# One float32 score product per head instead of three split ones, a later weight conversion, and two small passes on ScalarE

## The chip, the cores and the metric

The kernel runs on one core of a Trainium2 chip. The metric is the device time of one execution in microseconds. A core has a matrix engine (PE, whose weight loads are listed as PEld), a vector engine (DVE), a scalar engine (ACT), GpSimd (POOL), and SyncE (SP), which here issues the DMAs. Each engine works through its own queue in order.

## The reference

Attention with a compressive memory, and then two feed-forward layers, all in float32:

```
B, H, S, D = 4, 8, 576, 64
scores = q k^T / 8, causal;  a = softmax(scores);  local = a v
q_p = phi(q) = max(q, 0) + exp(min(q, 0))
mem_out = (q_p M_prev) / (q_p z_prev + 1e-6)
g = sigmoid(beta);  x = g * mem_out + (1 - g) * local     # 2304 tokens x 512
h = x w1_in (512 x 2048);  x = (h * cos(h)) w1_out
h = x w2_in (512 x 2048);  out = (h * tanh(softplus(h))) w2_out
```

## The kernel before

**Number format.** The kernel multiplies large matrices as pairs of float32r tiles, a rounded high part and the rest as a low part: a product a b is formed as aH bH + aH bL + aL bH, three matmuls into the same PSUM bank. Transposes, the memory product, a v and the sum with the memory's part are plain float32 products; the trace has two records (weight load and matmul) for each plain float32 product that isn't a transpose.

**Stages.** `attention` works on pairs of heads, 16 of them (4 batches of 4 pairs). The 576 query rows of a pair are 5 steps, i=0 to 4, so 80 steps in all, 20 per batch. In steps i=0 to 3 each head has its own score tile of 128 rows and 128(i+1) columns, and the two heads' operands lie in rows 0 to 63 and 64 to 127 of the array. Step 4 holds the last 64 rows of both heads in one tile (512 columns and 64 more). A step has three parts: `stage_a` (scores, softmax), two steps later `stage_b` (transposes of the attention tile), four steps later `stage_c` (a v, the sum, and the split into xH and xL, which are stored to DRAM with step 4).

**prep (L198 to L230)** runs for the next pair with step i=3. It loads k and q (kd, qd, from three shared `raw` tiles), rounds them to kh and qh, subtracts to kl and ql, and computes phi into `ph`: a minimum with 0 on DVE (L224), an exponential on ACT (L225), and one DVE pass (L226). `TURNS` gives the engine of each small operation in turn ("v" DVE, "a" ACT, "p" POOL), with own entries for the first batch (names that end in 0).

**stage_a (L232 to L275).** The three products per head (L246, L260), a custom DVE pass that adds the mask and takes the row's extreme (L248, L262, L265), the exponential on ACT that also gives the row sum sm (L251, L267), 1e-9 added to sm on DVE (L271), the reciprocal on DVE (L272), and the scaling of the tile on POOL (L274).

**The feed-forward** runs in three sequences: m1 (half of layer 1's hidden columns, blocks of 256 tokens), m2 (the other half) and m3 (layer 2). m1 is issued between attention's steps from the second batch on, by a pace (L580 to L586); what is left of it follows attention. In a unit the first product is L429, the second L487 (L496 in m3).

**The weight conversion.** Weights arrive in DRAM as 64 bit numbers. `to_f32` (L119 to L132) loads a piece of 512 KB into one of two staging tiles (`wst`) and turns it into float32 by one pass on POOL (L117), one on ACT (L126) and three on DVE (L127, L128, L131). `load_half` then rounds it into the high tile (ACT or POOL) and subtracts into the low tile (L161, POOL or DVE). The first half of layer 1 has 16 pieces. They are issued with attention's steps: after step s, int((s - CONV0 + 1) * CONVR) pieces, and at the latest before the units that need them (L584).

**Order.** The written order is the priority of a scheduler that simulates the engines and fixes each engine's queue, so that instructions can stand earlier or later than written; `issue_after` ties a piece behind the exponential of its step.

Of the kernel before, what the change touches and what calls it, by code (L numbers as in the profile page):

```python
# [9 lines left out]
F32 = mybir.dt.float32  # L10
F32R = mybir.dt.float32r
# [10 lines left out]
    mb=2, raw=3, aD=4, kh=3, kl=3, qs=2, vt=2, qt=1, ph=2, den=2, mo=4, xH=1, xL=3, sm=7, mn=2, at=8, aT=7, u=2, e=3, g=4, h=4, y=4, xb=3, yp=3, yh=2, yl=2, wst=2, S=6, T=8,  # L22
# [3 lines left out]
CONV0 = 2  # L26
CONVR = 1.5
# [6 lines left out]
    sc0="p", ql0="vp", kh0="a", kl0="vp", qh0="a", aT0="a",  # L34
    sc="p", ql="vp", kh="p", kl="ppv", ws="p", w0l="pv", w1l="vp", w2l="vp", w3l="vp", gl="p", gh="v", bh="a", mh="a",
    wh="ap", aT="av", yl="p", ml="vp", y0="v", y1="a", qh="a", aD="v",
# [7 lines left out]
def attention_moe_moe_kernel(  # L44
# [41 lines left out]
    make_identity(nc, ident)  # L86
    c_hpi = const.tile([P, 1], F32, name="c_hpi")
# [16 lines left out]
    def turn_of(kind, first=False):  # L104
        kind += "0" if first else ""
        n = counts.get(kind, 0)
        counts[kind] = n + 1
        return {"a": nc.scalar, "p": nc.gpsimd, "v": nc.vector}[TURNS[kind][n % len(TURNS[kind])]]
# [67 lines left out]
    def attention(ap, pools):  # L176
# [21 lines left out]
        def prep(b, p):  # L198
            st = {}

            kd = ap.tile([P, S + D], F32, tag="raw", name="kd", bufs=BUFS["raw"])
            kd = kd[:, :S]
            nc.sync.dma_start(kd, kT[b, p])
            qd = ap.tile([P, S + D], F32, tag="raw", name="qd", bufs=BUFS["raw"])
            nc.sync.dma_start(qd, qT[b, p])
            kh = ap.tile([P, S], F32R, tag="kh", name="kh", bufs=BUFS["kh"])
            kl = ap.tile([P, S], F32R, tag="kl", name="kl", bufs=BUFS["kl"])
            qh = ap.tile([P, S + D], F32R, tag="qh", name="qh", bufs=BUFS["qs"])
            ql = ap.tile([P, S + D], F32R, tag="ql", name="ql", bufs=BUFS["qs"])
            scaled("kh", kh, kd, first=b == 0)  # L210
            scaled("qh", qh, qd, first=b == 0)
            turn_of("kl", b == 0).tensor_tensor(kl, kd, kh.bitcast(F32), ALU.subtract)
            turn_of("ql", b == 0).tensor_tensor(ql, qd, qh.bitcast(F32), ALU.subtract)
            st["terms"] = ((qh, kh), (ql, kh), (qh, kl))
# [9 lines left out]
            nc.vector.tensor_scalar(ph, qt, 0.0, None, ALU.min)  # L224
            nc.scalar.activation(ph, ph, AF.Exp)  # L225
# [6 lines left out]
        def stage_a(b, p, i):  # L232
# [7 lines left out]
            if i < 4:  # L240
                N = P * (i + 1)
                sps = [bank("S", [P, SM], "sp") for _ in range(2)]
                for m, (q_, k_) in enumerate(st["terms"]):
                    for j, sp in enumerate(sps):
                        rows = slice(j * D, (j + 1) * D)
                        nc.tensor.matmul(sp[:, :N], q_[rows, q0:q0 + P], k_[rows, :N], start=m == 0, stop=m == 2)  # L246
# [7 lines left out]
            else:  # L254
                N = S
                at = ats[0]
                for k0, k1, w, name in ((0, SM, SM, "sp"), (SM, S, D, "sd")):
                    out = bank("S", [P, SM], name)
                    for m, (q_, k_) in enumerate(st["terms"]):
                        nc.tensor.matmul(out[:, :w], q_[:, q0:q0 + P], k_[:, k0:k1], start=m == 0, stop=m == 2)  # L260
                    if k0 == 0:
                        nc.vector.tensor_tensor_reduce(  # L262
                            at[:, :SM], out, mask[:, 0:SM], SSC, 3.0e38, ALU.add, ALU.min, mn[:, 0:1])
                    else:
                        nc.vector.tensor_tensor_reduce(  # L265
                            at[:, SM:], out[:, :D], mask2, SSC, mn[:, 0:1], ALU.add, ALU.min, mn[:, 1:2])
# [4 lines left out]
            nc.vector.scalar_tensor_tensor(sm, sm, 1e-9, sm, ALU.add, ALU.max)  # L271
# [404 lines left out]
```

## Time and profile before

| | |
|---|---|
| runs | 1080.91, 1084.23, 1088.42 us, median 1084.23 |
| profiled execution | 1085.15 us, its span 1083.4 us, mean granted clock 0.987 |
| PE, PEld busy | 1051.3 us (97 %), 901.1 us (83 %) |
| DVE, ACT, POOL busy | 531.2 us (49 %), 474.2 us (44 %), 434.3 us (40 %) |

The span is the time from the first to the last instruction. Busy times are unions over an engine's instructions; the sums of single lines can be larger, because neighbours overlap. Matmul ends are modelled, so a busy PE need not be PE at its peak. Attention ends at about 395 us, m1 at about 500 us, m2 at about 680 us.

### The profile page before, as it was taken

What the parts mean: (1) busy time and instruction counts of PE and PEld (TensorE: products, weight loads), DVE (VectorE), ACT (ScalarE), POOL (GpSimd) and SP (SyncE); (2) the same over time, 40 slices, a digit from 0 to 9 for tenths busy, and PEclk for the clock granted to TensorE, in tenths of its full rate; (3) what the DMA queues carried; (4) which work ended last, traced back from release to release, by engine and by line L of the source; (5) the groups of instructions that cost most, each with busy time, mean ns of one, the idle gap of its engine ahead of it and who ended that gap; (6) DMA issues with size and microseconds to landing.
All of it is one profiled execution on the core that took longest, in us unless ns stands there. A gap on an engine that the chain in (4) does not pass through costs nothing.

```text
span 1083.4 us, 17564 instructions
## 1 busy us (share of the span) xinstructions
PE 1051.3 (97%) x6672; PEld 901.1 (83%) x6672; DVE 531.2 (49%) x1246; ACT 474.2 (44%) x947; POOL 434.3 (40%) x454
## 2 busy tenths in 40 slices
PE   7888899999999999999999999999999999999998
PEld 5667688898989899998888889888888888888897
DVE  7999885647483657766657564655100000000000
ACT  6777475637273634334454454534422222232231
POOL 5988562435333335445556465544210101010100
PEclk9999799999999999999999999999999999999999
DMA  6566442424231246434456345633300200110010
GB/s 220 177 198 194 140 140 76 140 61 135 66 97 34 82 168 213 128 100 134 147 175 204 127 155 163 220 114 97 117 1 1 91 26 1 58 39 1 20 40 20
DMA packets 66373, 117.04 MB, mean 108 GB/s; under 512 B 5616, under 2 KB 25072, under 8 KB 66288
## 3 DMA queue, kind: packets, MB, share of 16 engines
q1 hardware_dynamic: 66288, 115.91, 32.7%
q8 instruction: 53, 0.87, 0.3%
q14 instruction: 32, 0.26, 0.1%
HBM read 87.58 MB, written 28.31 MB: 107 GB/s over the span
## 4 chain that ended last, share of the span: by engine, by line
PE 80%; DVE 7%; ACT 5%; DMA 4%; issue 2%; POOL 1%; SPq 0%; ACTq 0%; POOLq 0%; DVEq 0%
PE h L429 33%; PE y L496 18%; PE y L487 16%; PE o L333 3%; PE tp L306 3%; PE sp L246 3%; DMA wst<-in_w1i_dram 1%; DMA wst<-in_w1o_dram 1%; PE mp L286 1%; PE o L322 1%; DVE wst L131 1%; ACT at L251 1%; DVE wst L127 1%; DVE w L161 1%; DVE at L248 1%
## 5 line engine op out<-in xcount | busy, mean ns | idle before, releaser
L429 PE MATMUL h<-xbH,w 128*128 128x256 f32 (+1 forms) x1536 | 394.6, 338 | 0.2 <-DMA xbH<-xsH 0.2
L429 PEld LDWEIGHTS h<-xbH,w 128*128 128x128 f32 x1536 | 267.1, 190 | 33.6 <-issue 1.2
L429 PE MATMUL h<-xbL,w 128*128 128x256 f32 (+1 forms) x768 | 258.3, 337 | 0.0
L487 PE MATMUL y<-g,w 128*128 128x256 f32 (+1 forms) x1344 | 223.9, 321 | 1.7 <-DVE g L115 1.0
L487 PEld LDWEIGHTS y<-g,w 128*128 128x128 f32 x1344 | 195.7, 195 | 22.7 <-issue 3.3
L496 PE MATMUL y<-w,g 128*128 128x512 f32 x864 | 201.8, 389 | 0.0
L496 PEld LDWEIGHTS y<-w,g 128*128 128x128 f32 x864 | 161.9, 188 | 33.5
L401 DVE TENSOR_TENSOR g<-e,g 128x512 fp32r<-128x512 f32 x36 | 25.3, 702 | 288.9 <-ACT g L113 258.4
L429 PEld LDWEIGHTS h<-xbL,w 128*128 128x128 f32 x768 | 145.6, 190 | 15.5 <-DMA xbL<-xsL 0.3
L401 POOL TENSOR_TENSOR g<-e,g 128x512 fp32r<-128x512 f32 x36 | 47.6, 1322 | 275.6 <-ACT g L113 275.6
L274 POOL TENSOR_SCALAR at<-at,sm,omg 128x128 f32<-128x128 f32 (+2 forms) x144 | 110.2, 777 | 83.9 <-DVE sm L272 51.1
L393 ACT ACTIVATE e<-h 128x512 f32<-128x512 f32 x72 | 42.8, 595 | 216.7 <-PE h L429 216.3
L401 POOL TENSOR_TENSOR g<-u,g 128x512 fp32r<-128x512 f32 x72 | 102.3, 1438 | 70.7 <-DVE g L115 51.7
L117 POOL TENSOR_SCALAR wst<-wst 128x512 f32<-128x512 f32 x64 | 45.6, 713 | 116.7 <-DMA wst<-in_w2i_dram 40.6
L376 ACT ACTIVATE u<-h 128x512 int32<-128x512 f32 x72 | 42.3, 594 | 97.0 <-PE h L429 85.8
L251 ACT ACTIVATE at<-at,mn 128x128 f32<-128x128 f32 (+3 forms) x128 | 71.0, 556 | 30.7 <-DVE mn L248 28.3
L126 ACT ACTIVATE wst<-wst,c_seven 128x512 int32<-128x512 uint32 x64 | 48.9, 766 | 68.6 <-DMA wst<-in_w1o_dram 19.6
L306 PE MATMUL tp<-ident,at 128*128 128x128 f32 x384 | 67.3, 295 | 7.8 <-DVE xL L338 3.7
L377 DVE SCALAR_TENSOR_TENSOR u<-u,h 128x512 f32<-128x512 int32 x72 | 49.0, 683 | 51.0 <-ACT u L376 50.8
L127 DVE SCALAR_TENSOR_TENSOR wst<-wst 128x512 int32<-128x512 int32 x64 | 50.0, 781 | 41.6 <-ACT wst L126 20.4
L131 DVE TENSOR_TENSOR wst<-wst 128x512 int32<-128x512 int32 x64 | 68.4, 1070 | 1.1
L333 PE MATMUL o<-aT,vt 128*64 128x128 f32 (+1 forms) x896 | 63.9, 273 | 0.0
(94 smaller groups left out, 1251.5 us busy)
## 6 DMA issues: line engine op xcount, KB each, us to landing
wst<-in_w1i_dram SPq DMA_DIRECT2D x16, 512.0 KB, 3.9
wst<-in_w1o_dram SPq DMA_DIRECT2D x16, 512.0 KB, 4.1
wst<-in_w2i_dram SPq DMA_DIRECT2D x16, 512.0 KB, 3.7
wst<-in_w2o_dram SPq DMA_DIRECT2D x16, 512.0 KB, 3.6
qd<-in_qT_dram SPq DMA_DIRECT2D x16, 320.0 KB, 3.2
vt<-in_vn_dram SPq DMA_DIRECT2D x16, 320.0 KB, 3.3
xbH<-xsH SPq DMA_DIRECT2D x20, 256.0 KB, 4.6
xbL<-xsL SPq DMA_DIRECT2D x20, 256.0 KB, 4.4
```

What stands on the lines that cost most here:

```text
L126: nc.scalar.activation(lo, lo.bitcast(U32), AF.Relu, scale=-(2.0 ** -29), bias=c_seven)
L127: nc.vector.scalar_tensor_tensor(lo, hi, 3, lo, ALU.logical_shift_left, ALU.bitwise_or)
L131: nc.vector.tensor_tensor(dst, lo, hi, ALU.bitwise_xor)
L251: marks["act"] = nc.scalar.activation(at[:, :N], at[:, :N], AF.Exp, bias=mn[:, j:j + 1], scale=-1.0, accum_out=sm[:, j:j + 1]).ins
L274: turn_of("sc", b == 0).tensor_scalar(at[:, :N], at[:, :N], sm[:, j:j + 1], gates[j], ALU.mult, ALU.mult)
L306: nc.tensor.transpose(tp[:, c:c + P], at[:, c:c + P], ident)
L333: marks["pe"] = nc.tensor.matmul(o[j * D:(j + 1) * D, :n], st["vt"][:kk, c, j * D:(j + 1) * D], a, start=False, stop=c == i, skip_group_ch ...
L377: nc.vector.scalar_tensor_tensor(u, u.bitcast(I32), -TWO_PI, h, ALU.mult, ALU.add)
L401: turn_of(kind).tensor_tensor(gL, g, gH.bitcast(F32), ALU.subtract)
L429: nc.tensor.matmul(h[:, a * T:(a + 1) * T], w_[:, c, f0:f0 + P], x_[c], start=m == 0, stop=m == 3 * NC - 1)
L487: nc.tensor.matmul(y[e // per][:, cols], w_[:, f, es], g_, start=fst and m == 0 and e % per == 0, stop=lst and m == 2, skip_group_check=True)
L496: nc.tensor.matmul(y[t], g_[:, tsl], w_[:, f, :], start=fst and m == 0, stop=lst and m == 2, skip_group_check=True)
```

## The change

- Scores become one plain float32 product of q and k per head (steps 0 to 3) or per column range (step 4). The rounded and low tiles kh, kl, qh, ql and the operations that make them are gone. kd and qd are read by the matmuls themselves and have four tiles each; the three `raw` tiles are gone.
- The first weights' conversion starts with step 14 (CONV0) and issues 0.9 pieces a step (CONVR), instead of from step 2 with 1.5.
- phi's minimum, a DVE pass, becomes a Relu of -q on ACT, and the exponential takes the sign: exp(-relu(-q)).
- The 1e-9 on the row sum is added by an Identity pass with a bias tile on ACT, not by DVE.

```diff
-    mb=2, raw=3, aD=4, kh=3, kl=3, qs=2, vt=2, ...
+    mb=2, kd=4, qd=4, aD=4, vt=2, ...
-CONV0 = 2
-CONVR = 1.5
+CONV0 = 14
+CONVR = 0.9
 TURNS = dict(
-    sc0="p", ql0="vp", kh0="a", kl0="vp", qh0="a", aT0="a",
-    sc="p", ql="vp", kh="p", kl="ppv", ws="p", ...
+    sc0="p", aT0="a",
+    sc="p", ws="p", ...
...
+    c_eps = const.tile([P, 1], F32, name="c_eps")
+    nc.gpsimd.memset(c_eps, 1e-9)
...
-            kd = ap.tile([P, S + D], F32, tag="raw", name="kd", bufs=BUFS["raw"])
-            kd = kd[:, :S]
+            kd = ap.tile([P, S], F32, tag="kd", name="kd", bufs=BUFS["kd"])
             nc.sync.dma_start(kd, kT[b, p])
-            qd = ap.tile([P, S + D], F32, tag="raw", name="qd", bufs=BUFS["raw"])
+            qd = ap.tile([P, S + D], F32, tag="qd", name="qd", bufs=BUFS["qd"])
             nc.sync.dma_start(qd, qT[b, p])
-            kh = ap.tile([P, S], F32R, tag="kh", name="kh", bufs=BUFS["kh"])
-            kl = ap.tile([P, S], F32R, tag="kl", name="kl", bufs=BUFS["kl"])
-            qh = ap.tile([P, S + D], F32R, tag="qh", name="qh", bufs=BUFS["qs"])
-            ql = ap.tile([P, S + D], F32R, tag="ql", name="ql", bufs=BUFS["qs"])
-            scaled("kh", kh, kd, first=b == 0)
-            scaled("qh", qh, qd, first=b == 0)
-            turn_of("kl", b == 0).tensor_tensor(kl, kd, kh.bitcast(F32), ALU.subtract)
-            turn_of("ql", b == 0).tensor_tensor(ql, qd, qh.bitcast(F32), ALU.subtract)
-            st["terms"] = ((qh, kh), (ql, kh), (qh, kl))
+            st["q"], st["k"] = qd, kd
...
-            nc.vector.tensor_scalar(ph, qt, 0.0, None, ALU.min)
-            nc.scalar.activation(ph, ph, AF.Exp)
+            nc.scalar.activation(ph, qt, AF.Relu, scale=-1.0)
+            nc.scalar.activation(ph, ph, AF.Exp, scale=-1.0)
...
-                for m, (q_, k_) in enumerate(st["terms"]):
-                    for j, sp in enumerate(sps):
-                        rows = slice(j * D, (j + 1) * D)
-                        nc.tensor.matmul(sp[:, :N], q_[rows, q0:q0 + P], k_[rows, :N], start=m == 0, stop=m == 2)
+                for j, sp in enumerate(sps):
+                    rows = slice(j * D, (j + 1) * D)
+                    nc.tensor.matmul(sp[:, :N], st["q"][rows, q0:q0 + P], st["k"][rows, :N], start=True, stop=True)
...
-                    for m, (q_, k_) in enumerate(st["terms"]):
-                        nc.tensor.matmul(out[:, :w], q_[:, q0:q0 + P], k_[:, k0:k1], start=m == 0, stop=m == 2)
+                    nc.tensor.matmul(out[:, :w], st["q"][:, q0:q0 + P], st["k"][:, k0:k1], start=True, stop=True)
...
-            nc.vector.scalar_tensor_tensor(sm, sm, 1e-9, sm, ALU.add, ALU.max)
+            nc.scalar.activation(sm, sm, AF.Identity, bias=c_eps)
```

## Rows read from the trace of the kernel before

**Rows 1.** Windows: start:end, length, busy us (instructions) by engine, granted clock, DMA share, GB/s.

```profile
0.00:20.00 20.00, 11.95 (x53) 9.12 (x54) 13.55 (x46) 11.90 (x28) 11.04 (x36) 1.00 0.74 249
20.00:160.00 140.00, 124.53 (x1045) 98.89 (x1045) 129.44 (x401) 96.72 (x262) 105.35 (x113) 0.94 0.53 167
160.00:400.00 240.00, 236.72 (x2071) 210.28 (x2072) 137.57 (x460) 125.82 (x291) 86.98 (x106) 0.98 0.28 90
500.00:1084.00 584.00, 579.78 (x2738) 487.48 (x2737) 180.31 (x232) 201.69 (x313) 179.11 (x152) 1.00 0.26 87
```

**Rows 2.** Chain that ended last, 0 to 160 us: start us, us, what.

```profile
24.68 0.86 ACT at L267 x2
...
68.00 1.69 DVE wst L131
...
141.07 0.87 ACT at L267 x2
```

**Rows 3.** Timeline of ACT near 59 us: start us, us, instruction, shapes, count.

```profile
59.09 0.79 ACT L267 ACTIVATE at<-at,mn 128x576 f32<-128x576 f32 x1
```

**Rows 4.** Lines on DVE, 0 to 160 us: count | busy us, mean ns | idle before.

```profile
L131 DVE TENSOR_TENSOR wst<-wst 128x512 int32<-128x512 int32 x16 | 16.2, 1010 | 0.0
L271 DVE SCALAR_TENSOR_TENSOR sm<-sm 128x2 f32<-128x2 f32 (+1 forms) x40 | 16.1, 403 | 1.9 <-ACT at L251 1.9
L127 DVE SCALAR_TENSOR_TENSOR wst<-wst 128x512 int32<-128x512 int32 x16 | 12.0, 750 | 0.7 <-POOL wst L117 0.6
L128 DVE TENSOR_SCALAR wst<-wst 128x512 int32<-128x512 int32 x16 | 9.6, 599 | 0.0
L161 DVE TENSOR_TENSOR w<-wst,w 128x512 fp32r<-128x512 f32 x8 | 9.1, 1137 | 0.5 <-POOL w L117 0.5
L213 DVE TENSOR_TENSOR ql<-qd,qh 128x640 fp32r<-128x640 f32 x5 | 5.3, 1063 | 0.1
L224 DVE TENSOR_SCALAR ph<-qt 128x576 f32<-128x576 f32 x10 | 5.2, 518 | 1.2 <-DMA qt<-in_qp_dram 1.2
L212 DVE TENSOR_TENSOR kl<-kd,kh 128x576 fp32r<-128x576 f32 x4 | 3.4, 857 | 1.0 <-ACT kh L113 1.0
```

**Rows 5.** Lines on ACT, 0 to 160 us.

```profile
L113 ACT ACTIVATE qh<-qd 128x640 fp32r<-128x640 f32 x10 | 7.3, 731 | 3.5 <-PE sd L260 3.4
L225 ACT ACTIVATE ph<-ph 128x576 f32<-128x576 f32 x10 | 6.7, 674 | 0.4 <-DVE ph L224 0.2
L94 ACT ACTIVATE gate<-gate 128x8 f32<-128x8 f32 x1 | 0.2, 208 | 0.7 <-DMA gate<-in_beta_dram 0.7
```

**Rows 6.** Lines on POOL, 0 to 160 us.

```profile
L212 POOL TENSOR_TENSOR kl<-kd,kh 128x576 fp32r<-128x576 f32 x7 | 10.8, 1536 | 8.0 <-ACT kh L113 7.8
L213 POOL TENSOR_TENSOR ql<-qd,qh 128x640 fp32r<-128x640 f32 x5 | 8.0, 1594 | 0.4 <-ACT qh L113 0.4
```

**Rows 7.** Timeline of PE, 53 to 62 us: scores, and float32 products in column halves.

```profile
53.77 0.44 PE L333 MATMUL o<-aT,vt 128*64 128x128 f32 x4
...
56.24 0.66 PE L333 MATMUL o<-aT,vt 128*64 128x128 f32 x8
...
56.99 0.28 PE L246 MATMUL sp<-kh,ql 64*128 64x128 f32 x2
57.10 0.28 PE L246 MATMUL sp<-kl,qh 64*128 64x128 f32 x2
...
60.05 0.41 PE L246 MATMUL sp<-kh,ql 64*128 64x512 f32 x2
60.28 0.41 PE L246 MATMUL sp<-kl,qh 64*128 64x512 f32 x2
```

**Rows 8.** Tile wst, 0 to 160 us: durations min/median/max ns, first and last start us.

```profile
L161 DVE TENSOR_TENSOR w<-wst,w x8: 668/680/3995, 29.9 to 141.2; 128x512 fp32r<-128x512 f32 x8
```

**Rows 9.** Waits of SP's DMA queue, 0 to 160 us: total us, times, longest.

```profile
SPq L123 <- POOL w L161: 13.8, 6, 5.3
...
SPq L203 <- POOL ql L213: 6.4, 2, 3.4
```

More of the change, by code (lines that the diff above doesn't have):

```diff
@@ L21 @@
 BUFS = dict(
-    mb=2, raw=3, aD=4, kh=3, kl=3, qs=2, vt=2, qt=1, ph=2, den=2, mo=4, xH=1, xL=3, sm=7, mn=2, at=8, aT=7, u=2, e=3, g=4, h=4, y=4, xb=3, yp=3, yh=2, yl=2, wst=2, S=6, T=8,
+    mb=2, kd=4, qd=4, aD=4, vt=2, qt=1, ph=2, den=2, mo=4, xH=1, xL=3, sm=7, mn=2, at=8, aT=7, u=2, e=3, g=4, h=4, y=4, xb=3, yp=3, yh=2, yl=2, wst=2, S=6, T=8,
 )
@@ L33 @@
 TURNS = dict(
-    sc0="p", ql0="vp", kh0="a", kl0="vp", qh0="a", aT0="a",
-    sc="p", ql="vp", kh="p", kl="ppv", ws="p", w0l="pv", w1l="vp", w2l="vp", w3l="vp", gl="p", gh="v", bh="a", mh="a",
-    wh="ap", aT="av", yl="p", ml="vp", y0="v", y1="a", qh="a", aD="v",
+    sc0="p", aT0="a",
+    sc="p", ws="p", w0l="pv", w1l="vp", w2l="vp", w3l="vp", gl="p", gh="v", bh="a", mh="a",
+    wh="ap", aT="av", yl="p", ml="vp", y0="v", y1="a", aD="v",
 )
```

## The prediction

> **What bounds the kernel now.** I read the profile by stretches first, because its whole-span shares mix stages with different limits. The windows [rows 1] show that from 160 us to the end the matrix engine PE is the limit: 237 of 240 us busy up to 400 us, then 100 %, with DVE, ACT and POOL far below. Before 160 us it is another machine: between 20 and 160 us DVE is busy 129.4 of 140 us (92 %), PE 124.5, POOL 105, ACT 97. Busy PE time is a modelled latency there; the mean granted clock of that stretch, 0.94, is a mixture of the two levels, 1.2 and 2.4 GHz. So PE starves for a good part of this stretch, and what starves it is DVE.
>
> The chain of waits tells the same [rows 2]: it runs through DVE's pieces of the weight conversion (L131 at 68 us, 1.69 us, is one of these links). It also gives the pace of attention: the exponential of step i=4 of the first pair starts at 24.7 us, that of the seventh pair at 141.1 us, so (141.1 - 24.7)/6 = 19.4 us a pair. The timeline of ACT puts the third pair's, which is step 14, at 59.1 us [rows 3].
>
> What fills DVE up to 160 us is in its lines [rows 4]: four lines of conversion make 16.2 + 12.0 + 9.6 + 9.1 = 46.9 us. The four lines that the change takes off DVE make 16.1 (L271) + 5.3 (L213) + 5.2 (L224) + 3.4 (L212) = 30.0 us. Line sums overlap on the engine: all DVE lines of the stretch together make 172 us where the windows give 13.55 + 129.44 = 143, so I scale a line sum by 143/172 = 0.83.
>
> **The change, part by part.**
>
> *DVE.* 30.0 x 0.83 = 25 us leave it in the first 160 us, and 143 - 25 = 118 us are left for the same work. The conversion is 46.9 x 0.83 = 39 of them; the rest, less some 4 us that belong to the first cosine tiles, is (118 - 39 - 4)/8 = 9.4 us a pair, where it was 12.5.
>
> *POOL* loses its share of kl and ql, 10.8 + 8.0 us [rows 6], and kh besides. POOL was 105 of 140 us busy, not the limit; I count nothing for it. The work that hides it is DVE's.
>
> *ACT* [rows 5] loses qh (7.3 us) and in the first batch kh. It gains ten Relu passes, priced as the exponential over the same tile, 674 ns, so 6.7 us, and 40 Identity passes over one or two columns. The trace has no such pass of two columns; the nearest row, 8 columns without a bias tile, is 208 ns, so 8.3 us. From below it cannot be less than nothing, from above it is the 403 ns that DVE took, 16 us. I take 8.3. Net +8 us on 108, on an engine that was 97 of 140 us busy: hidden behind DVE and PE as long as these are the later ones; uncovered it would cost up to 8 us. The Identity follows the exponentials on ACT's own queue, so DVE's reciprocal still waits for ACT once, as L271 did; behind it on ACT stand the next step's exponentials and copies, each later by 0.2 us.
>
> *PE.* Two heads lie in the two row halves of the array. Before, three products run for both at once: the second and third pair of records start 0.11 us apart at 128 columns and 0.23 us at 512 [rows 7]; for 256 and 384 I take 0.12 and 0.17, by columns. Three products over i=0 to 3 make 3 x (0.11 + 0.12 + 0.17 + 0.23) = 1.89 us, and i=4 adds 3 x (0.23 + 0.11) = 1.02. A float32 product is two records. Float32 for two halves at once appears only in L333, for two column halves: four records in 0.44 us, eight in 0.66 [rows 7], so 0.11 us for two records side by side over 128 columns, 0.86 ns a column, twice float32r's price. Row halves then cost 2 x (0.11 + 0.22 + 0.33 + 0.44) = 2.20 us, and i=4 2 x (0.44 + 0.11) = 1.10. That is 3.30 against 2.91: PE gets 0.39 us more a pair. For the eight pairs after 160 us, where PE is the limit, 3.1 us; for the first eight it lies beside DVE. If the two heads did not run side by side at all, steps 0 to 3 would cost 4.40 instead of 2.20.
>
> Eight records in 0.66 us are four slots (0.16 + 2 x 0.11 + 0.27 for the last one's latency), and four in 0.44 us are two slots: the second half's first record does not wait for the first half's second. The Trainium skill says otherwise: "TensorE: Matmul & The Clock Gate", Part 3, section "The mechanism", has matmuls start strictly in program order. By that rule the two records of a head would keep the other head's first one waiting; the trace of L333 disagrees (0.44 us, where three slots would make 0.55). The sum goes by the rows, and the rule's result is a rival below.
>
> *The conversion, moved.* All 16 pieces stay, from step 14 instead of step 2. On the chip they did not keep the written pace: DVE's L161, which every second piece has, runs eight times from 29.9 to 141.2 us [rows 8], (141.2 - 29.9)/14 = 8 us a piece, because only two staging tiles (wst) exist and each queues at DVE, ACT and POOL. Their DMA issues on SP wait for a free tile, e.g. 13.8 us for POOL's L161 [rows 9]; behind them on SP stand the next pairs' loads, the stores of xH and xL and the loads of x. They are moved past three pairs' loads on that queue. In exchange SP's waits for a free raw tile (6.4 us for ql among them [rows 9]) go, as kd and qd get four tiles each; I count both at nothing.
>
> *The sum.* Up to step 14 DVE now has 9.4 us a pair and no longer binds. What is late next is PE with ACT: by the windows ACT had 97/140 x 19.4 = 13.4 us of work a pair, PE 124.5/140 x 19.4 = 17.3, latency, some feed-forward and half clock included. I take 16 us, between the two and nearer to PE. The 2.9 pairs up to step 14 then save 2.9 x 3.4 = 10 us: step 14 at 49 us. By then DVE has done 2.9 x 9.4 + 2 = 29 of its 118 us. The other 89 us, at the 92 % that it reached before, take 96 us: the state of 160 us is reached at 145 us. That is 15 us early; less 3.1 us on PE leaves 12. The profiled execution has 1085.15 us around a span of 1083.4; 1085.15 - 12 = 1073. It lies 0.9 us over the median of the runs, 1084.23, so I put the new median at 1072.
>
> The bounds: at DVE 80 % busy the 89 us take 111, nothing is gained and PE's 3.1 us remain, 1088. At the other end PE's recorded idle time before 160 us, 8.0 + 15.5 = 23.5 us [rows 1], is the most that a faster feed can give at the same clock: 1085 - 23.5 + 3 = 1065, and some 7 us less if PE also stays at 2.4 GHz (the 0.94 granted means 2 x 0.06 x 140 = 17 us at 1.2 GHz, half of them lost), 1058.
>
> **The rivals.**
>
> *The gain is eaten by the later conversion.* DVE idles a third of the first 49 us and must then do the same 39 us beside attention. If two staging tiles still give 8 us a piece, the last ends at 49 + 16 x 8 = 177 us, 36 us later than now, and the first feed-forward units, which could fill PE, move back with it. For it: the pieces' pace was set by their queueing. Against: attention then has DVE to itself and is PE work as well. 1080 to 1090.
>
> *PE stands at a late weight (the other side).* PE's queue is in order. A feed-forward product that is issued before attention's next step, and whose weight piece comes late, holds up attention behind it. Before, no such wait is seen; pieces were done well ahead of the units, which need batch 0's output: 24.7 + 3 x 19.4 us and four more steps, some 98 us. It decides once such waits exceed the 12 us gained; the four units' pieces, each late by a staging turn of 8 us, would be 32 us: 1085 - 12 + 32 = 1105.
>
> *Float32 heads don't run side by side.* In strict order three slots instead of two add 0.11 + 0.22 + 0.33 + 0.44 = 1.1 us a pair, 9 to 18 us over eight or sixteen pairs: 1081 to 1090. With no overlap at all it is 2.2 us a pair, 18 to 35 us: 1090 to 1107. For it: no row shows float32 in row halves. Against: L333 in column halves, and float32r in row halves.
>
> *PE is fed fully*, 1058 to 1065, if DVE's and POOL's relief shortens each other's passes too (L131 took 1010 ns on average up to 160 us).
>
> **How the numbers follow.** A measurement here tells about 1 % from no change: 1073.4 is the border to faster, 1095.1 to slower. Chances: the forecast (1065 to 1080) 0.48, the eaten gain 0.22, float32 one after the other 0.10, PE at a late weight 0.08, fully fed 0.12. Likeliest 1072. Faster: a little over half of the forecast and the fully fed case, 0.28 + 0.12 = 0.40. Slower: the late weight and most of the no-overlap case with the tails, 0.17. The rest, 0.43, lies within 1 %. The forecast's own range is 1065 to 1080; the range for 8 in 10 leaves out most of the two slow rivals, 1058 to 1092.
>
> **What would show it.** Right: DVE's share in 20 to 50 us well below 90 %, steps of a pair some 16 us apart up to step 14, the feed-forward running without gaps from about 145 us; score products in two slots of 0.44 us at 512 columns for both heads; after 160 us the same work with 0.4 us more a pair. Wrong: waits of PE for w tiles, score products of the two heads one after the other, or conversion pieces that end after 170 us with PE idle in between.

## The result and the profile after

The changed kernel takes 1069.68 us (median of four runs, 1068.55 to 1072.91); the kernel before, beside it on the same chip, 1084.56 us (1080.91 to 1088.42). The ratio is 0.9864 [0.9838, 0.9889], 1.4 % faster. The forecast was 1072 us in a range of 1058 to 1092: the measured time lies inside the range, 2.3 us below the forecast. The question that is left is whether the time went where the forecast said. The profiled execution of after has a span of 1068.0 us (1083.4 before) at a mean granted clock of 0.993 (0.987).

First the windows of after, by the stretches of [rows 1] and two more; the columns are those of [rows 1].

```profile
0.00:20.00 20.00, 10.98 (x46) 6.45 (x47) 8.58 (x39) 11.16 (x32) 8.26 (x37) 0.90 0.89 304
20.00:160.00 140.00, 131.73 (x1073) 96.73 (x1074) 109.26 (x373) 110.68 (x314) 84.68 (x100) 0.98 0.52 169
160.00:400.00 240.00, 235.82 (x2003) 200.98 (x2003) 123.98 (x398) 128.52 (x317) 74.27 (x95) 0.99 0.32 103
400.00:500.00 100.00, 99.75 (x726) 94.83 (x726) 73.49 (x109) 42.24 (x62) 51.52 (x51) 1.00 0.49 166
...
20.00:60.00 40.00, 40.00 (x309) 27.34 (x311) 23.37 (x95) 31.84 (x102) 12.11 (x19) 0.96 0.35 113
```

Between 20 and 160 us DVE fell from 129.4 to 109.3 us and POOL from 105.4 to 84.7, ACT rose from 96.7 to 110.7, and PE from 124.5 to 131.7. Between 20 and 60 us DVE is down to 23.4 of 40 us, where it was busy for 39.4 before. DVE is no longer full there; whether its time still costs something is asked by a run below.

Then DVE's lines up to 160 us, in the columns of [rows 4]: three of the four lines of conversion, and the reciprocal that now follows the Identity pass.

```profile
L133 DVE TENSOR_TENSOR wst<-wst 128x512 int32<-128x512 int32 x16 | 12.5, 784 | 0.1
L129 DVE SCALAR_TENSOR_TENSOR wst<-wst 128x512 int32<-128x512 int32 x16 | 11.6, 723 | 2.8 <-POOL wst L119 2.3 <-ACT wst L128 0.6
...
L263 DVE RECIPROCAL sm<-sm 128x2 f32<-128x2 f32 (+1 forms) x42 | 6.4, 157 | 8.2 <-ACT sm L262 8.1
L163 DVE TENSOR_TENSOR w<-wst,w 128x512 fp32r<-128x512 f32 x8 | 5.6, 699 | 1.2 <-POOL w L119 1.2
```

The same 16 pieces take DVE 39.2 us (with L130's 9.5) where they took 46.9 [rows 4], although nothing in them was changed: L131, now L133, went from 1010 to 784 ns and L161, now L163, from 1137 to 699.

ACT's two new lines:

```profile
L262 ACT ACTIVATE sm<-sm,c_eps 128x2 f32<-128x2 f32 (+1 forms) x42 | 11.9, 288 | 0.3
...
L217 ACT ACTIVATE ph<-qt 128x576 f32<-128x576 f32 x11 | 7.4, 674 | 2.5 <-DMA qt<-in_qp_dram 2.5
```

And PE's timeline near 200 us, the score products of both heads (L238), of a step 4 (L251), and L324, which was L333 in [rows 7].

```profile
197.03 1.13 PE L238 MATMUL sp<-kd,qd 64*128 64x512 f32 x4
...
198.51 0.44 PE L324 MATMUL o<-aT,vt 128*64 128x128 f32 x4
...
199.59 1.02 PE L251 MATMUL sp<-kd,qd 128*128 128x512 f32 x2
200.45 0.33 PE L251 MATMUL sd<-kd,qd 128*128 128x64 f32 x2
...
201.58 0.49 PE L238 MATMUL sp<-kd,qd 64*128 64x128 f32 x4
```

Two records of 512 columns occupy PE for 200.45 - 199.59 = 0.86 us, 0.43 each. Four records of both heads end after 1.13 us, that is two slots of 0.43 and another 0.27 that does not grow with the columns (three slots would be 1.56); at 128 columns 0.49 = 2 x 0.11 + 0.27. In the trace the second head's first record starts 0.007 us after the first head's. The heads run side by side.

**One measure for all kernels.** A busy PE says little here, so I price each matmul record at the interval at which such records follow one another without a gap (float32r 0.23 us at 512 columns, 0.12 at 256; transposes 0.11; float32 0.11 per 128 columns, half where two run side by side), call the sum work and the rest of the span idle; what a stretch at the lower clock takes beyond these prices counts as idle too. The borders are the starts of the exponential of step 4 of the third pair (E3, step 14), the eighth (E8) and the sixteenth (E16, attention's end). For example, after: work 975.8, idle 84.9 up to E16 and 7.2 behind it, together 1067.9. In the table idle stands as up to E8 / E8 to E16 / behind E16, in us. The last four columns are of one profiled execution of each kernel, "clock" is its mean granted clock. Two of these executions lie far from their kernel's median: scores_alone's is 4.7 us above it, dve_dose's 5.1 us below; the others are within 2.2 us.

| kernel | median (before beside it) | ratio | E3, E8, E16 | idle | work | clock |
|---|---|---|---|---|---|---|
| before | 1084.56 | | 59.1, 157.5, 380.9 | 65.3 / 39.0 / 9.1 | 970.0 | 0.987 |
| after | 1069.68 (1084.56) | 0.9864 [0.9838, 0.9889] | 53.9, 150.3, 366.9 | 51.9 / 33.0 / 7.2 | 975.8 | 0.993 |
| scores_alone | 1077.69 (1087.14) | 0.9914 [0.9888, 0.9941] | 56.5, 154.9, 377.1 | 59.9 / 33.9 / 11.0 | 975.8 | 0.986 |
| early_conv | 1067.84 (1087.14) | 0.9810 [0.9764, 0.9856] | 58.5, 146.5, 365.7 | 51.6 / 32.3 / 6.9 | 975.8 | 0.989 |
| small_on_dve | 1080.22 (1087.14) | 0.9933 [0.9903, 0.9962] | 55.2, 161.5, 381.1 | 66.2 / 31.6 / 6.4 | 975.8 | 0.987 |
| no_eps | 1077.31 (1087.14) | 0.9897 [0.9853, 0.9940] | 53.1, 150.7, 369.5 | 54.9 / 31.4 / 11.9 | 975.8 | 0.990 |
| dve_dose | 1090.45 (1085.09) | 1.0024 [0.9991, 1.0058] | 57.1, 157.7, 377.9 | 60.7 / 35.3 / 11.7 | 975.8 | 0.993 |
| pool_dose | 1089.57 (1085.96) | 1.0029 [1.0011, 1.0048] | 52.7, 159.9, 382.4 | 63.7 / 36.8 / 10.9 | 975.8 | 0.983 |
| double_scores | 1129.06 (1085.09) | 1.0412 [1.0362, 1.0463] | 64.2, 182.9, 428.0 | 61.7 / 33.5 / 6.4 | 1027.9 | 0.989 |
| conv_spread | 1067.92 (1085.09) | 0.9845 [0.9796, 0.9895] | 55.5, 144.5, 364.3 | 49.4 / 33.0 / 6.5 | 975.8 | 0.997 |
| early_wst3 | 1075.25 (1085.09) | 0.9904 [0.9873, 0.9934] | 55.6, 142.9, 362.2 | 47.9 / 32.4 / 15.9 | 975.8 | 0.992 |
| spread_noeps | 1067.49 (1085.96) | 0.9828 [0.9788, 0.9868] | 57.4, 146.1, 365.4 | 51.5 / 31.8 / 6.4 | 975.8 | 0.992 |
| spread_phi_pool | 1086.07 (1085.96) | 0.9994 [0.9973, 1.0015] | 57.2, 158.3, 376.8 | 63.0 / 31.9 / 12.0 | 975.8 | 0.990 |
| spread_scale_dve | 1074.89 (1085.94) | 0.9891 [0.9854, 0.9927] | 57.4, 148.0, 366.6 | 52.2 / 32.5 / 12.7 | 975.8 | 0.993 |

So the change removed 13.4 us of idle up to E8, 6.0 from there to E16 and 1.9 behind it, and added 5.8 us of work: -15.5, the difference of the spans.

A part of this idle is the clock. At 1.2 GHz matmul records take twice their time: in double_scores those of step 4 at 512 columns follow each other every 0.85 us near 20 us, where the granted clock is 0.50, and every 0.43 us near 42 us, where it is 1.00. A span loses (1 - granted clock) of its length in this way: some 14 us before and 7 after, an estimate from the granted clock of each stretch. So about 7 of the 21.3 us of idle that went are no longer lost to the lower level: 8.5 us before and 5.1 after up to E8, 5.1 and 1.7 from there to E16. Between E8 and E16 before has three stretches of 3.4 us at 0.50, after has one.

```profile
157.49:380.93 223.44, 220.16 (x1910) 193.99 (x1909) 132.74 (x451) 120.45 (x284) 85.06 (x103) 0.98 0.28 88
215.20:218.60 3.40, 3.40 (x18) 3.40 (x18) 2.05 (x13) 1.95 (x8) 3.17 (x3) 0.50 0.46 131
```

```profile
150.28:366.94 216.66, 212.48 (x1789) 176.83 (x1789) 114.93 (x395) 126.53 (x320) 65.70 (x88) 0.99 0.27 88
```

The first two windows are of before, the third of after. Why the clock fell where it did was not tested, and it differs between executions of one kernel (0.986 to 0.998 for scores_alone), so differences of a few us in the idle column are no evidence by themselves.

### The profile page after: what moved, and what is told of

It reads as the page before. It is cut to its first block, busy times and chain, and to the rows that moved or that the text cites. A ratio compares the mean times of both kernels' runs of the same rounds, so it can differ in the third digit from the quotient of the medians.

```text
span 1068.0 us, 17139 instructions
## 1 busy us (share of the span) xinstructions
PE 1042.6 (98%) x6512; PEld 873.7 (82%) x6512; DVE 490.7 (46%) x1136; ACT 485.8 (45%) x1023; POOL 391.6 (37%) x425
## 4 chain that ended last, share of the span: by engine, by line
PE 92%; ACT 2%; DVE 2%; DMA 2%; issue 1%; POOL 1%; SPq 0%; DVEq 0%; POOLq 0%; ACTq 0%
PE h L420 37%; PE y L478 20%; PE y L487 18%; PE o L324 5%; PE sp L238 4%; PE tp L297 4%; PE o L313 2%; PE mp L277 1%; PE sp L251 1%; DMA qt<-in_qp_dram 1%; DMA wst<-in_w1i_dram 1%; DVE at L240 1%; ACT at L243 1%; DMA vt<-in_vn_dram 1%; POOL at L265 0%
## 5 line engine op out<-in xcount | busy, mean ns | idle before, releaser
L478 PE MATMUL y<-g,w 128*128 128x256 f32 (+1 forms) x1344 | 221.5, 319 | 4.4 <-ACT aT L115 4.2
L478 PEld LDWEIGHTS y<-g,w 128*128 128x128 f32 x1344 | 193.1, 192 | 30.8 <-issue 9.4
L487 PEld LDWEIGHTS y<-w,g 128*128 128x128 f32 x864 | 161.9, 188 | 33.5
L265 POOL TENSOR_SCALAR at<-at,sm,omg 128x128 f32<-128x128 f32 (+2 forms) x144 | 102.7, 723 | 134.4 <-DVE sm L263 119.2
L243 ACT ACTIVATE at<-at,mn 128x128 f32<-128x128 f32 (+3 forms) x128 | 70.9, 555 | 28.2 <-DVE mn L240 26.8
L129 DVE SCALAR_TENSOR_TENSOR wst<-wst 128x512 int32<-128x512 int32 x64 | 53.9, 843 | 37.7 <-POOL wst L119 31.3
L297 PE MATMUL tp<-ident,at 128*128 128x128 f32 x384 | 63.9, 285 | 5.6 <-DVE den L281 2.2
L240 DVE CUSTOM_DVE_ANT_0 at<-sp,mask 128x128 f32<-128x128 f32 (+3 forms) x128 | 59.3, 482 | 17.6 <-PE sp L238 16.0
L133 DVE TENSOR_TENSOR wst<-wst 128x512 int32<-128x512 int32 x64 | 66.1, 1035 | 1.2
L324 PE MATMUL o<-aT,vt 128*64 128x128 f32 (+1 forms) x896 | 64.5, 272 | 1.7 <-ACT aT L115 1.5
```

Of the source, the lines that this page charges most:

```text
L129: nc.vector.scalar_tensor_tensor(lo, hi, 3, lo, ALU.logical_shift_left, ALU.bitwise_or)
L133: nc.vector.tensor_tensor(dst, lo, hi, ALU.bitwise_xor)
L240: nc.vector.tensor_tensor_reduce(at[:, :N], sp[:, :N], mask[:, SM - q0:SM - q0 + N], SSC, 3.0e38, ALU.add, ALU.min, mn[:, j:j + 1])
L243: marks["act"] = nc.scalar.activation(at[:, :N], at[:, :N], AF.Exp, bias=mn[:, j:j + 1], scale=-1.0, accum_out=sm[:, j:j + 1]).ins
L265: turn_of("sc", b == 0).tensor_scalar(at[:, :N], at[:, :N], sm[:, j:j + 1], gates[j], ALU.mult, ALU.mult)
L297: nc.tensor.transpose(tp[:, c:c + P], at[:, c:c + P], ident)
```

## The experiments

**Which part brings it.** Four kernels, each after with one part taken back.

scores_alone: the new scores, but the conversion's old pace and both small passes on DVE.

```diff
-CONV0 = 14
-CONVR = 0.9
+CONV0 = 2
+CONVR = 1.5
...
-    c_eps = const.tile([P, 1], F32, name="c_eps")
-    nc.gpsimd.memset(c_eps, 1e-9)
...
-            nc.scalar.activation(ph, qt, AF.Relu, scale=-1.0)
-            nc.scalar.activation(ph, ph, AF.Exp, scale=-1.0)
+            nc.vector.tensor_scalar(ph, qt, 0.0, None, ALU.min)
+            nc.scalar.activation(ph, ph, AF.Exp)
...
-            nc.scalar.activation(sm, sm, AF.Identity, bias=c_eps)
+            nc.vector.scalar_tensor_tensor(sm, sm, 1e-9, sm, ALU.add, ALU.max)
```

> The changed kernel with the old conversion pace (from step 2, 1.5 a step) and the two small passes back on DVE: of the change only the float32 scores and the missing split are left. Theory A (DVE's work before 160 us sets the gain): DVE loses only kl and ql, 8.7 us by line sums, some 7 us of 143, and PE gains some 6 us of work, so about 1080 us, within 5 us of before. Theory B (the gain comes from the shorter way to the first product and from POOL's 24 us, not from DVE): most of the 15 us is already here, 1068 to 1073 us.

Measured 0.9914, 9.4 us in the medians. The profiled executions show less: idle up to E16 falls by 10.5 us (104.3 to 93.8), the added work takes 5.8 of them back, and the span goes from 1083.4 to 1080.6 us; but this execution is the slowest of the nine, at a granted clock of 0.986 where their median is 0.995. So the scores alone bring about 9 us, by the interval of the ratio between 6 and 12, which lies between the two theories.

early_conv: only the conversion's pace is taken back (CONV0 = 2, CONVR = 1.5).

> The changed kernel with the old conversion pace alone (from step 2, 1.5 a step). Theory A: DVE, idle for a third of the first 55 us in the changed kernel, gets that time back; its 118 us at 92 % end some 8 to 10 us earlier, 1060 to 1063 us. Theory C (the later start is itself part of the gain, because the pieces stand in the way of attention's steps while there is no feed-forward that could use them): slower than the changed kernel by 5 us or more, 1075 us.

Measured 0.981. It stands beside scores_alone on one chip, and the two differ by the small passes alone: 1077.69 - 1067.84 = 9.9 us, idle up to E16 from 93.8 to 83.9. Against after (0.9864) the intervals overlap, and it is not slower; the moved conversion brings nothing. The gain over after that the first theory expected, 1060 to 1063 us, is not there either.

small_on_dve: only the small passes are taken back, all of scores_alone's diff but the conversion's pace.

> The changed kernel with the row sum's 1e-9 and phi's minimum back on DVE. DVE gets 21 us by line sums back in the first 160 us, some 18 us, and ACT is rid of 19 us. Theory A: DVE binds between 55 and 150 us, so 8 to 14 us slower than the changed kernel, 1078 to 1084 us. Rival (ACT, now 111 of 140 us busy before 160 us, binds as much as DVE): no slower than the changed kernel, 1067 to 1072 us.

Measured 0.9933; 66.2 us of idle up to E8 where after has 51.9. By this pair the small passes bring 0.9933 - 0.9864, 7 us by the ratios and 12 in the spans, inside the range that the first theory gave. Against scores_alone it differs by the later conversion alone, and is 2.5 us slower.

no_eps: the Identity pass is gone, DVE's reciprocal takes the row sum as it is.

```diff
-    c_eps = const.tile([P, 1], F32, name="c_eps")
-    nc.gpsimd.memset(c_eps, 1e-9)
...
-            nc.scalar.activation(sm, sm, AF.Identity, bias=c_eps)
```

> The changed kernel without the Identity pass that adds 1e-9 to the row sum. The addition is left out; the row sum holds exp(0) = 1, so in float32 the sum is the same number. ACT is rid of 80 passes of 0.29 us, 12 us of them before 160 us, and the chain from the exponential to the reciprocal is shorter by one pass. Theory A: DVE binds where anything but PE does, so 0 to 3 us faster, 1067 to 1070 us. Rival (ACT binds up to step 14): 4 to 8 us faster, 1062 to 1066 us.

Measured 0.9897, idle up to E16 86.3 where after has 84.9: 80 passes of 0.29 us fewer on ACT bring nothing. The kernel loses 4.7 us behind E16, where it has no pass more or less than after, and so lies above both expected ranges; this loss is looked at in the last section.

**What bounds the first stage.** Three doses of work on one engine each, added to after, none of it read by anything else.

dve_dose: one pass over kd in each of the 80 steps.

```diff
             nc.vector.reciprocal(sm, sm)
+            scr = ap.tile([P, S], F32, tag="scr", name="scr", bufs=2)
+            nc.vector.tensor_scalar(scr, st["k"], 0.0, None, ALU.min)
```

> The changed kernel with one more DVE pass in every step, a minimum over kd (128x576) into a scratch tile that nothing reads; ACT and the chain from score to attention tile stay as they are. The nearest row, L224 of the kernel before, took 0.52 us, so 40 passes before 160 us are 21 us by line sums, as much as the two small passes were on DVE. Theory A (DVE's occupancy before 160 us): 7 to 12 us slower than the changed kernel, 1077 to 1082 us, about where the kernel with the small passes on DVE was. Rival (those passes cost through their place in the chain from the exponential to the attention tile, not through DVE's time): within 3 us of the changed kernel, 1067 to 1073 us.

pool_dose: two subtractions for each pair, on POOL, like those that made kl and ql.

```diff
             st["q"], st["k"] = qd, kd
+            for _ in range(2):
+                scr = ap.tile([P, S], F32, tag="scr", name="scr", bufs=2)
+                nc.gpsimd.tensor_tensor(scr, kd, qd[:, :S], ALU.subtract)
```

> The changed kernel with two more POOL passes per pair (kd minus qd, 128x576, into a scratch tile that nothing reads). One such subtraction took POOL 1.5 us in the kernel before, so POOL gets back 3 us a pair, what kh, kl and ql cost it there; DVE, ACT and PE keep their work. Theory A as it was forecast (POOL's relief is worth nothing): within 2 us of the changed kernel, 1068 to 1072 us. Rival (POOL's passes lengthen DVE's, so POOL's relief is part of the gain): the conversion passes on DVE grow back from 0.78 us (the last of the three) towards 1.01 us, and the kernel is 4 to 9 us slower, 1074 to 1079 us.

The doses up to 160 us, by line, and what pool_dose does to two of DVE's passes; then the passes of L222 by tile ph (durations min/median/max) and one wait on DVE. L243 is after's L240, L222 its L219.

```profile
L265 DVE TENSOR_SCALAR scr<-kd 128x576 f32<-128x576 f32 x57 | 27.4, 511 | 2.8 <-DMA kd<-in_kT_dram 2.8
```

```profile
L210 POOL TENSOR_TENSOR scr<-kd,qd 128x576 f32<-128x576 f32 x24 | 35.9, 1513 | 7.6 <-DMA kd<-in_kT_dram 7.6
...
L243 DVE CUSTOM_DVE_ANT_0 at<-sp,mask 128x128 f32<-128x128 f32 (+3 forms) x65 | 30.4, 478 | 11.9 <-PE sp L241 4.3 <-ACT at L246 4.0 <-ACT sm L265 1.9
L222 DVE SCALAR_TENSOR_TENSOR ph<-qt,ph 128x576 f32<-128x576 f32 x10 | 12.6, 1259 | 0.3 <-ACT ph L221 0.3
...
L222 DVE SCALAR_TENSOR_TENSOR ph<-qt,ph x10: 745/828/3592, 10.4 to 143.4; 128x576 f32<-128x576 f32 x10
...
DVE sm L266 <- POOL scr L210: 4.1, 2, 2.2
```

Both take the whole gain away: 1.0024 and 1.0029. That is more than either theory had foreseen for either run. In all, DVE's dose is 40.3 us and costs 96.0 - 84.9 = 11.1 us of idle up to E16, 0.28 us for each; POOL's is 47.1 us and costs 15.6, 0.33 for each. The rest of the two losses lies behind E16 (11.7 and 10.9 us, after has 7.2). These prices are rough. By the ratios, and with what is lost behind E16, the doses cost 17 and 18 us, 0.4 for each us on either engine; the execution behind DVE's 0.28 lies 5.1 us below its median; and 10.2 of POOL's 15.6 us are time at the lower clock (17.0 us up to E16 where after lost 6.8). Which engine's us costs more was not told apart. Neither engine is the bound in the sense that its time is paid in full, and neither is covered. A chain in which work passes from PE to DVE to ACT to DVE to POOL and back, and pays a part of whatever stands in any of these queues, would fit this; no run tests the chain as such.

double_scores: every float32 score product is issued twice into the same bank.

```diff
-                    nc.tensor.matmul(sp[:, :N], st["q"][rows, q0:q0 + P], st["k"][rows, :N], start=True, stop=True)
+                    for _ in range(2):
+                        nc.tensor.matmul(sp[:, :N], st["q"][rows, q0:q0 + P], st["k"][rows, :N], start=True, stop=True)
...
-                    nc.tensor.matmul(out[:, :w], st["q"][:, q0:q0 + P], st["k"][:, k0:k1], start=True, stop=True)
+                    for _ in range(2):
+                        nc.tensor.matmul(out[:, :w], st["q"][:, q0:q0 + P], st["k"][:, k0:k1], start=True, stop=True)
```

> The changed kernel with every float32 score product made twice into the same bank, the second over the first, so the result is the same. PE gets 3.3 us more a pair (two slots of two columns' time for both heads), 53 us in all. Theory A: the eight pairs after 160 us pay in full, 26 us, the first eight only in part, since PE has 54 us of idle time before 160 us: 1096 to 1110 us. Rival (PE binds from the start in the changed kernel): the full 53 us, 1123 us. If the heads' products do not run side by side, more than 53 us.

Measured 1.0412, (1.0412 - 0.9864) x 1085 = 59 us more for 52.1 us more work. That is above both expected ranges, but not because the heads' products ran one after the other: eight records of both heads at 512 columns end after 1.99 us, four slots of 0.43 and the 0.27. Nothing of the added work is hidden, in the first eight pairs either: E8 moves by 32.6 us, where 8 x 3.3 = 26 us of work came in. The 6.6 us beyond that are what this execution loses more to the lower clock up to E8, 11.9 us where after lost 5.1. Each us of PE's work is paid.

**When the conversion should run.**

conv_spread: from step 2, but half a piece a step (CONV0 = 2, CONVR = 0.5).

> The changed kernel with the conversion from step 2 on but only 0.5 pieces a step, so that the last is written with step 33, just before the units that need it. Theory A: DVE's work is the same and spread evenly, no idle time early and no crowd late, so as fast as the early conversion or faster, 1060 to 1067 us. Rival (start and pace of the conversion do not matter, since PE has attention's own work to do either way): within 3 us of the changed kernel, 1067 to 1073 us.

early_wst3: early_conv with a third staging tile (`wst=3`).

> The changed kernel with the old conversion pace (from step 2, 1.5 a step) and three staging tiles instead of two, in the space that the split tiles left. If the pieces' pace is set by two staging tiles, the last piece ends well before 114 us (it ended there with two), DVE is denser up to then and free after, and the time is that of the early conversion or a little less, 1060 to 1068 us. If pieces that come quicker stand in attention's way, step 14 comes later than 58.5 us and the time is 1070 us or more.

L163 on DVE, which every second piece has, in after, early_conv, conv_spread and early_wst3 (tile wst up to 160 us: durations min/median/max, then first and last start):

```profile
L163 DVE TENSOR_TENSOR w<-wst,w x8: 675/686/751, 65.0 to 149.1; 128x512 fp32r<-128x512 f32 x8
```

```profile
L163 DVE TENSOR_TENSOR w<-wst,w x8: 665/882/1116, 21.2 to 114.1; 128x512 fp32r<-128x512 f32 x8
```

```profile
L163 DVE TENSOR_TENSOR w<-wst,w x8: 676/702/1148, 34.8 to 126.5; 128x512 fp32r<-128x512 f32 x8
```

```profile
L163 DVE TENSOR_TENSOR w<-wst,w x8: 676/746/1109, 23.9 to 93.8; 128x512 fp32r<-128x512 f32 x8
```

The last piece ends between 94 and 149 us, and idle up to E16 goes with it only from 80.3 to 84.9 us. When the conversion starts hardly matters, as long as it is done before the units need it. early_wst3 has the least idle in attention, 80.3 us, and gives it back: 15.9 us behind E16, with waits like these between 400 and 500 us (total, times, longest), of which conv_spread has none there. Of the 15.9 us 3.4 are time at the lower clock. That the pieces come quicker and stand in the way of attention's steps, for which its range of 1070 us and more stood, is not what happened: step 14 came at 55.6 us, before early_conv's 58.5.

```profile
PE y L478 <- POOL g L392: 2.4, 1, 2.4
PE y L478 <- DVE g L117: 1.7, 1, 1.7
```

**Can more be moved?** Three kernels on top of conv_spread.

spread_noeps: without the Identity pass, as no_eps.

> The spread conversion (from step 2 at 0.5 a step) without the Identity pass that adds 1e-9 to the row sum. The addition is left out; the row sum holds exp(0) = 1, so in float32 the sum is the same number. The same omission in the changed kernel gave no gain. If that was because ACT's passes cost nothing: within 3 us of the spread conversion, 1065 to 1071 us. If it was only another order that the scheduler chose there, the 12 us that ACT is rid of before 160 us show here as 3 to 8 us: 1060 to 1065 us.

Measured 0.9828 beside conv_spread's 0.9845: no difference, and idle up to E16 83.3 against 82.4. The Identity pass costs nothing that these runs can tell.

spread_phi_pool: phi's last pass, one on DVE, becomes two on POOL.

```diff
-            nc.vector.scalar_tensor_tensor(ph, qt, 0.0, ph, ALU.max, ALU.add)
+            nc.gpsimd.tensor_scalar(qt, qt, 0.0, 1.0, ALU.max, ALU.mult)
+            nc.gpsimd.tensor_tensor(ph, qt, ph, ALU.add)
```

> The changed kernel with the conversion spread from step 2 at 0.5 a step, and phi's last DVE pass (0.83 us, 9 us before 160 us) made as two passes on POOL (a maximum, an addition, some 0.8 and 1.5 us). Theory A (DVE's occupancy before 160 us): 5 to 9 us faster than the spread conversion alone, 1059 to 1063 us. Rival (POOL's passes cost DVE as much as they take from it, or phi comes later in the chain): 1066 to 1072 us.

Measured 0.9994, above both expected ranges: the whole gain is gone. POOL's two lines up to 160 us, and PE's longest wait there:

```profile
L219 POOL TENSOR_SCALAR qt<-qt 128x576 f32<-128x576 f32 x10 | 21.8, 2179 | 4.6 <-ACT ph L217 3.6 <-POOL w L163 1.0
L220 POOL TENSOR_TENSOR ph<-qt,ph 128x576 f32<-128x576 f32 x10 | 14.6, 1465 | 0.0
...
PE mp L278 <- POOL ph L220: 8.9, 2, 7.8
```

POOL takes 36.4 us for what DVE did in about 9 (the first of its two passes takes 2.2 us where 0.8 had been expected), and the idle up to E8 rises by 13.6 us.

spread_scale_dve: the tile's scaling alternates between POOL and DVE (`sc0="pv", sc="pv"`).

> The changed kernel with the conversion spread from step 2 at 0.5 a step, and every second scaling pass of the attention tiles on DVE instead of POOL. Before 160 us POOL then loses half of these passes, some 30 us by line sums, and DVE gains some 36 passes; 512 columns with two factors have a near row in the conversion's mask on DVE (0.4 to 0.5 us against POOL's 0.97), so 13 us. By the doses (20 us for 27 us on DVE's lines at most, 19 us for 36 us on POOL's) that is -16 and +9: 4 to 9 us faster than the spread conversion, 1059 to 1064 us. Rival (DVE is the only limit before 160 us, POOL's dose hurt through the order of its queue alone): 6 to 10 us slower, 1074 to 1078 us.

The windows of conv_spread and, below, of spread_scale_dve:

```profile
20.00:160.00 140.00, 133.05 (x1090) 96.17 (x1090) 111.08 (x376) 108.92 (x314) 85.71 (x100) 0.99 0.52 168
```

```profile
20.00:160.00 140.00, 134.75 (x1082) 97.04 (x1081) 123.36 (x412) 109.67 (x316) 59.32 (x66) 0.97 0.54 173
```

POOL loses 26 us and DVE gains 12, and the idle up to E16 stays, 84.7 against 82.4 us. By the doses' prices it should have fallen by 0.33 x 26.4 - 0.28 x 12.3 = 5 us, so these prices do not carry over even to this kernel. The time lies in the rival's range, but not for its reason, since DVE's 12 us cost nothing up to E16. The 0.9891 is worse than conv_spread's 0.9845 by what is lost behind E16 (12.7 us against 6.5), where the scaling doesn't exist any more. No kernel that was run beats after clearly: early_conv, conv_spread and spread_noeps overlap with it. The converse of scores_alone, the old scores with the new rest, was not tried; what the small passes would bring there stays open. So does how much of scores_alone's gain comes from work taken off POOL and DVE, and how much from products that no longer wait for rounding and subtracting or from the eight tiles of kd and qd: no run has these apart.

## Why the prediction was right, and where its steps were not

The forecast's account, term by term, against the table:

| term | forecast | measured |
|---|---|---|
| idle gone up to E8 (the state of 160 us reached earlier) | -15 | -13.4 |
| float32 scores on PE | +3.1 | +5.8 |
| idle in pairs 9 to 16 | 0 | -6.0 |
| behind attention | 0 | -1.9 |
| sum | -12 | -15.5 |

**Right, or nearly.** DVE's busy time for the work that before has behind it at 160 us was forecast at 118 us. After reaches E8 7.2 us earlier than before, and up to 152.8 us DVE is busy for 112.3 us: the conversion's passes got shorter, which the forecast did not have. (That it is 8.6 + 109.3 = 117.8 up to 160 us is more work in as much time.) The pace up to step 14 was forecast at 16 us a pair; the exponentials of the first and the third pair start at 21.19 and 53.88 us, 16.35 a pair. Step 14 is at 54 and not at 49 us, for another reason: the 19.4 us that the forecast set against its 16 were the mean over six pairs, and the first pairs were not as slow, (59.09 - 24.68)/2 = 17.2 us [rows 2, 3]. Up to there 5.2 us were won, 3.5 of them in the first pair, and not 10.

```profile
21.19 0.77 ACT L258 ACTIVATE at<-at,mn 128x576 f32<-128x576 f32 x1
...
53.88 0.78 ACT L258 ACTIVATE at<-at,mn 128x576 f32<-128x576 f32 x1 [0.24 <-DVE mn L256]
```

The price of the scores on PE came out as worked out from L333: slots of 0.43 us at 512 and 0.11 at 128 columns, and 5.8 us of work counted in all, where 16 x 0.39 is 6.2. That the heads would not run side by side, the third rival, is refuted by L238's 1.13 us. The Trainium skill's rule in "TensorE: Matmul & The Clock Gate", Part 3, section "The mechanism", that matmuls start strictly in program order, would make it 1.56 if the two records of a head stand one behind the other in PE's queue; the trace disagrees with that, as it did for L333 before. It shows when the records start but not their order in the queue, so the rule itself is not refuted.

**The rivals of the conversion fell.** The first needed 8 us a piece; after has (149.1 - 65.0)/14 = 6.0, and the last piece at 149 us, not 177. Of the waits of PE up to 160 us the only one of a feed-forward product is for x, not for a weight, so the second fell too:

```profile
PE h L420 <- DMA xbL<-xsL: 1.5, 1, 1.5
```

But the delay brings nothing either: early_conv and conv_spread, which convert early, are at least as fast. What the forecast gained by keeping DVE free up to step 14 is gained without it.

**"POOL's relief: nothing" was wrong.** That was the step "POOL was 105 of 140 us busy, not the limit; I count nothing for it", and pool_dose refutes it: 47.1 us given back to POOL cost 15.6 us of idle. A likely reason why scores_alone gains at all is that the rounding and subtracting that it removes lay mostly on POOL, and that POOL's work also lengthened DVE's: the four conversion lines, unchanged there, take DVE 40.4 us where they took 46.9. The change took 30 us of lines off DVE [rows 4] and, by the windows, 23.5 off POOL up to 160 us (kl, ql [rows 6] and kh above all); 0.28 x 30 + 0.33 x 23.5 = 16 us (a rough estimate from the two doses) where 13.4 were measured. The forecast got 15 from DVE alone, by calling it the bound and charging all of it. On this account its size was right by luck: too much for DVE and nothing for POOL nearly cancel.

**"For the first eight it lies beside DVE" was wrong.** double_scores shows PE's work paid in full from the first pair on. The term is 5.8, not 3.1.

**"Nothing gained after 160 us" was wrong.** Idle from E8 to E16 is 39.0 us before and between 31.4 and 33.9 in all kernels with the new scores except those with a dose. It comes with the scores, not with the small passes (31.6 with them on DVE). Of the 6.0 us between before and after, 3.4 are time at the lower clock. Without such time, by the same estimate, before has 33.9 us there, after 31.3, pool_dose 33.2 and dve_dose 35.3. PE also changes shape less often, 291 runs of matmul records of one shape before and 270 after between E8 and E16; what makes the 2.6 us that are left stays open.

**Identity** was put at 0.208 us and takes 0.288, 11.9 us up to 160 instead of 8.3. No gain came from leaving it out (no_eps, spread_noeps): it is covered, as the forecast had it. The Trainium skill's "ScalarE: Activation LUTs", section "What ACT_TABLE_LOAD costs", gives 280 ns and 0.833 ns an element for an activation with a bias tile, 282 ns for two columns by an estimate from it; the trace agrees with 288.

**Fully fed PE**, the fourth rival, is where the surplus points: DVE's passes did get shorter with less POOL work beside them (L131 from 1010 to 784 ns), but 51.9 us of idle stay up to E8.

## What to carry to other kernels

In a stage where PE waits for a chain through several engines, do not take the fullest engine for the only one that costs time: add a dose of unread work to each engine (here 0.3 to 0.4 us for a us of DVE or POOL, about 1 for PE), leave a pass out where that is possible (0 for ACT's Identity), and move work from the engines that cost time to the free one. Such prices say where to look; they are not exact enough to add up (spread_scale_dve). A matmul that was added here was not hidden by PE's idle time. Compare kernels by the idle of each stage, and by the clock that was granted in it, before reading a cause out of the total, because what is lost in the next stage (here up to 9 us) belongs to another cause.

## What the runs showed of the hardware

POOL's passes lengthen DVE passes that read two operands from SBUF, and not those that read their tile from PSUM. From after to pool_dose the pass of phi (two SBUF tiles) goes from 833 to 1259 ns, with one of 3592 (its median goes from 751 to 828), and the conversion's L133 from 784 to 943. The mask pass over the scores (PSUM) stays, 473 and 478 ns. Up to 160 us the passes of L133 during which POOL ran nothing take 0.68 us each, in after (4) and in pool_dose (5) alike; the others take 0.82 and 1.09 us on average. The small pass that the change moved to ACT shows it best: before, L271 takes 0.15 us in the 9 cases in which POOL stood still and 0.48 us on average in the 31 others, so some 10 of its 16.1 us [rows 4] were not its own work.

```profile
L240 DVE CUSTOM_DVE_ANT_0 at<-sp,mask 128x128 f32<-128x128 f32 (+3 forms) x68 | 31.3, 473 | 9.6 <-PE sp L238 8.2 <-POOL at L265 1.1
...
L219 DVE SCALAR_TENSOR_TENSOR ph<-qt,ph 128x576 f32<-128x576 f32 x11 | 9.2, 833 | 2.6 <-ACT ph L218 2.6
```

The row of L271 before, with its shortest, median and longest pass:

```profile
L271 DVE SCALAR_TENSOR_TENSOR sm<-sm x40: 134/289/1281, 11.8 to 159.2; 128x2 f32<-128x2 f32 x32, 128x1 f32<-128x1 f32 x8
```

The Trainium skill has this in "SBUF — State Buffer", section "Who interferes with whom": DVE and GpSimd share a pair of ports under an exclusive lock, and a DVE instruction with two SBUF inputs contends for it where one with at most one, outside DVE's two-port modes, does not. The trace agrees by these numbers; the reciprocal, with one input of two columns, takes 0.16 us in after with and without POOL beside it. L130, with one SBUF input of 512 columns, is lengthened as well, from 0.42 us without POOL beside it to 0.62 on average with it. How much of the 15.6 us comes from this and how much from POOL's own queue was not told apart.

The idle behind attention is 6.4 to 7.2 us in six of the kernels and 9.1 to 15.9 in the others (before among them), for edits that do not touch that stage. It moves the total by some 5 us, as much as some of the edits. The order of the instructions does not explain it: in dve_dose, pool_dose and spread_phi_pool (10.9 to 12.0 us) PE, DVE, ACT and POOL work through the same instructions in the same order behind E16 as in after (7.2); only in early_wst3 does the order there differ much. What does differ is how long ACT waits for weight pieces from DRAM over the whole run, here in after and then in dve_dose:

```profile
ACT wst L128 <- DMA wst<-in_w1o_dram: 9.8, 6, 4.8
```

```profile
ACT wst L128 <- DMA wst<-in_w1o_dram: 25.3, 13, 4.0
```

For the pieces of this one matrix it is 4.0 to 9.8 us in the six kernels and 18.5 to 25.3 in the seven others with two staging tiles. Why the pieces come later in these stays open.
